# One transfer in place of four for a tile of tokens, two in place of three for a block of first weights, and the last tile stored by column halves

## The chip, the core and the metric

The kernel runs on one core of a Trainium2 chip. A core has five engines that work side by side, each from its own instruction queue in program order: TensorE (matrix products; PE and PEld in the profile), VectorE (DVE), ScalarE (ACT), GpSimd (POOL) and SyncE (SP), which here only issues transfers. Transfers between the chip's memory (DRAM) and the on-chip memory (SBUF, 128 partitions) are issued from SP's, ACT's and POOL's queues and carried out by 16 DMA engines that all queues share. Products land in PSUM, from where ScalarE and VectorE fetch them. The metric is the device time of one execution in microseconds (us), lower is better.

## What is computed

The input `x` has 2048 tokens of 576 channels. It is normalized per token, and the output is the sum of x, a state-space convolution over the tokens, and a feed-forward layer:

```python
xn = _layernorm(x, axis=-1)
return x + _A_ref(xn, A_re, A_im, B_re, B_im, C_re, C_im, log_dt, Dskip) + _B_ref(xn, w1, w2)

def _B_ref(x, w1, w2):                       # w1: 576 x 4608, w2: 4608 x 576
    h = jnp.einsum("bsd,df->bsf", x, w1)
    h = _silu(h)
    return jnp.einsum("bsf,fd->bsd", h, w2)

def _A_ref(u, A_re, ...):                    # per channel d
    K = jnp.einsum("dn,dnl,dn->dl", Cc, jnp.exp(logdA[:, :, None] * l), dB).real
    y = irfft2(rfft2(u padded) * rfft2(K padded))[..., :L]      # causal convolution of length 2048
    return y + u * Dskip
```

All of it is float32. The kernel forms float32 products from three products of rounded parts (a high half and a low half of each operand: hi x hi, hi x lo, lo x hi).

## The kernel before

**Tiles.** The 2048 tokens are 16 tiles of 128 tokens, numbered j; tile j has the tokens whose number is j modulo 16, and the token's other digits choose the partition. Two tiles (j, j + 1) make a pair, whose rows of 2 x 576 numbers are contiguous in DRAM. Tiles 0 to 7 are half 0, tiles 8 to 15 half 1; four tiles are a block b of 512 tokens.

**x.** `load_x` brings a pair in by four transfers of 32 partitions each (`quarters`), the first pair by eight, of one tile and 32 partitions each, on SP's and ACT's queues by turns. `norm` takes mean and variance on VectorE (`bn_stats`, line 188), the reciprocal root on POOL (line 193), and writes xn (line 197). `turned` and `put_xt` transpose xn on TensorE (line 122), ScalarE writes the high halves `xh` (line 123) and VectorE the low halves `xl` (line 125). xn also goes to DRAM (`dxn`, POOL, line 240), from where the convolution reads it back.

**Feed-forward.** The 4608 hidden features are chunks of 4 x 128. `load_w1` brings the 576 x 256 weights of two of them in three transfers: the rows 0 to 511 (line 257), and the last 64 rows twice, to the lower and the upper 64 partitions (lines 258 and 259). `split_w1` makes `w1h` on ScalarE (line 279) and `w1l` on VectorE (line 281); `load_w2` and `split_w2` do the same for w2 (lines 288, 297, 299). `up` forms the hidden product for one set of 128 features and one block in `ph` (lines 311 to 313), then SiLU and the two halves `gh`, `gl` (lines 319 to 321). `down` multiplies with w2 (line 341) and adds to `acc`, which holds x at first (line 346). The last blocks of half 1 are formed with fewer products (`wino_ffn`, whose weights are split at line 385).

**Convolution.** It runs as side work beside the feed-forward, a piece after each step (`weave`): normalized x is spread and transformed (`spread`, into `d1u`), the kernel K is generated from tables (`kgen`), and per frequency block both are multiplied (`spectral`) and transformed back (`conv`). In half 0 the finished tiles are stored to the output by POOL and the convolution's part is later added in DRAM by accumulating stores (`last` in `tail`). In half 1 `conv` puts its part into the same PSUM banks as `down`.

**Order.** A scheduler lays out each engine's queue from the program by its own estimate of durations, under orders that the code adds (`behind`: not ahead of a given instruction). Each queue is then served strictly in order. Buffers come from rotating pools; a transfer into a buffer waits until the buffer's last reader is done.

**The ends.** At the start, SP issues x, w1 and w2 in program order, ACT's queue carries half of the first x pair's transfers and half of the first w1 block. At the end, the pairs 8, 10 and 12 and the tiles 14 and 15 of half 1 are stored by SP and ACT, two quarters each, as their last additions finish.

Of the kernel before, what the change touches and what calls it, by code (L numbers as in the profile page):

```python
# [13 lines left out]
ALU = mybir.AluOpType  # L14
# [8 lines left out]
NJ = 16  # L23
NKT = 4
HD = D // 2
# [16 lines left out]
def kernel(  # L42
# [21 lines left out]
    nc = tc.nc  # L64
# [2 lines left out]
    WINO_C = 2  # L67


    xv = x.rearrange("b (n q2 q1 j) d -> q1 q2 n (b j) d", q2=2, q1=2, j=NJ)  # L70
    ov = out.rearrange("b (n q2 q1 j) d -> q1 q2 n (b j) d", q2=2, q1=2, j=NJ)

    def quarters(v, engines):

        for q in range(4):
            yield slice(32 * q, 32 * q + 32), v[q // 2, q % 2], engines[q % len(engines)]

    dram = ctx.enter_context(tc.tile_pool(name="dram", bufs=1, space=DRAM))
    d1u = dram.tile([32 * P, D], F32, name="d1u")
# [10 lines left out]
    s4 = None  # L90
# [19 lines left out]
    acc = {}  # L110
# [21 lines left out]
    pairs = {}  # L132
    held = []
    pins = {}
    wino = {}

    def behind(ins):
        return tc.issue_after(ins) if ins is not None else nullcontext()

    def spread(up):  # L140

        s1 = up.tile([P, 2, P], F32R, name="s1", bufs=1)
        nc.gpsimd.dma_start(s1, cs1)
        for j in range(NJ):
            src = up.tile([P, D], F32, tag="xr", name="xr")
            nc.sync.dma_start(src, dxn[:, j])
            for m in range(2):
                lo, hi = slice(64 * m, 64 * m + 64), slice(64 - 64 * m, 128 - 64 * m)
                u1 = up.tile([P, D], F32, tag="u1", name="u1")
                sp = up.tile([P, D], F32R, tag="sp", name="sp")  # L150
                nc.scalar.copy(sp[lo, :], src[lo, :])
                nc.vector.tensor_sub(sp[hi, :], src[lo, :], sp[lo, :])
                for h in range(2):
                    hs = slice(h * HD, (h + 1) * HD)
                    pu = pss.tile([P, 512], F32, tag="pss", name="pu")
                    nc.tensor.matmul(pu[:, :HD], s1[:, 0, :], sp[:, hs], start=True, stop=False)
                    nc.tensor.matmul(pu[:, :HD], s1[:, 1, :], sp[:, hs], start=False, stop=True)
                    nc.scalar.copy(u1[:, hs], pu[:, :HD])  # L158
                nc.gpsimd.dma_start(  # L159
                    d1u.rearrange("(p m j) d -> m j p d", m=2, j=NJ)[m, j], u1)  # L160
                yield j

    def load_x(j, pool, tag, engines):

        t = pool.tile([P, 2, D], F32, tag=tag, name=f"{tag}{j}")
        for i in range(j, j + 2, 1 if j == 0 else 2):
            for ps, v, eng in quarters(xv, engines):
                if j == 0:
                    eng.dma_start(t[ps, i], v[:, i])
                else:  # L170
                    eng.dma_start(t[ps], v[:, j:j + 2])
        pairs[j] = t
        return t[:, 0, :], t[:, 1, :]

    def store(t, j, engines, **more):

        for ps, v, eng in quarters(ov, engines):
            eng.dma_start(v[:, j:j + 2] if len(t.shape) > 2 else v[:, j], t[ps], **more)

    def norm(p0, js, xs):  # L180

# [60 lines left out]
    def ffn():  # L242
# [7 lines left out]
        def load_w1(half, c, t):  # L250

            f = c * FT + t
            first = half == 0 and c == 0
            r1 = (pa if first and t else w1x if t and w1x else wp).tile([P, 5, 2 * P], F32, tag="w1r", name="w1r", bufs=1)
            for eng, a, e in ((nc.scalar, 0, P), (nc.sync, P, 2 * P)) if first and t == 0 else ((nc.sync, 0, 2 * P),):
                fs = slice(f * P + a, f * P + e)
                eng.dma_start(r1[:, 0:4, a:e], w1[0:512, fs].rearrange("(k p) f -> p k f", p=P))
                eng.dma_start(r1[0:64, 4, a:e], w1[512:576, fs])
                pins["load"] = eng.dma_start(r1[64:128, 4, a:e], w1[512:576, fs]).ins
            R1[half, c, t] = r1  # L260

        def need_w1(half, c, t):
            if (half, c, t) not in R1:
                load_w1(half, c, t)

        def next_w1(half, c, t):
            new = (half, c + 1) if c + 1 < NCH else (half + 1, 0)
            if w1x and new < (1, WINO_C):
                load_w1(*new, t)
# [53 lines left out]
        def down(blk, jj, terms=None):  # L323
            half, c, b = blk
            j = 8 * half + 4 * b + jj
            js = slice(jj * P, (jj + 1) * P)
            if half == 1 and c == NCH - 1 and jj % 2 == 0:
                pools = (((ps2, "ps2"), (pss, "pss")), ((pss, "pss"),) * 2) if jj == 0 else (((ps2, "ps2"),) * 2, ((ps1, "ps1"),) * 2)
                for i in range(2):
                    begun[j + i] = [pool.tile([P, 512], F32, tag=tag, name="po") for pool, tag in pools[i]]  # L330
                conv((j, j + 1), (begun[j], begun[j + 1]))
                for i in range(2):
                    conv_load(j + i + AHEAD)
            terms = terms or [(G[blk, t], W2[half, c, t]) for t in range(FT)]
            for h in range(2):
                hs = slice(h * HD, (h + 1) * HD)
                po = begun[j][h] if j in begun else ps2.tile([P, 512], F32, tag="ps2", name="po")
                n = 0
                for gs, ws in terms:
                    for g, w in ((0, 0), (0, 1), (1, 0)):  # L340
                        pins["pe"] = nc.tensor.matmul(po[:, :HD], gs[g][:, js], ws[:, w, hs],  # L341
                                                      start=n == 0 and j not in begun, stop=n == 3 * len(terms) - 1,
                                                      skip_group_check=j in begun).ins
                        n += 1
                with tc.high_priority():
                    nc.vector.tensor_add(acc[j][:, hs], po[:, :HD], acc[j][:, hs])  # L346
            if half == 0 and c == NCH - 1:
                if j % 2:
                    store(pairs[j - 1], j - 1, (nc.gpsimd,))
                    acc[7 + j], acc[8 + j] = load_x(7 + j, accp, "acc", (nc.gpsimd,))  # L350

        def next_xt(b):
# [65 lines left out]
        for i, blk in enumerate(plain[:-1]):  # L418
            half, c, b = blk
            later = True  # L420
            new = (half, c + 1) if c + 1 < NCH else (half + 1, 0)
            more = new < (1, WINO_C)
# [559 lines left out]
    def tail():  # L982

        def last(j):
            y = yp.tile([P, 2, D], F32, tag="yt", name="yt", bufs=2)
            py = [[pool.tile([P, 512], F32, tag=tag, name="py") for pool, tag in pools]
                  for pools in (((ps2, "ps2"), (pss, "pss")), ((pss, "pss"),) * 2)]
            conv((j, j + 1), py)
            for i in range(2):
                for h in range(2):  # L990
                    nc.scalar.copy(y[:, i, h * HD:(h + 1) * HD], py[i][h][:, :HD])
                conv_load(j + i + AHEAD)
            store(y, j, (nc.gpsimd,), accum_op=ALU.add)

        steps = [(tail_at[0] + j * tail_at[1], conv_load, j) for j in range(AHEAD)]
        steps += [(tail_at[2] + j * tail_at[3], last, j) for j in range(0, 8, 2)]
        for at, f, j in sorted(steps, key=lambda v: v[0]):
            yield at
            with behind(pins["load"]):
                f(j)  # L1000
# [24 lines left out]
    def conv_load(j):  # L1025
        if j < NJ:
            yss[j] = yp.tile([P, 4, HD], F32, tag="ys", name="ys", bufs=AHEAD)
            for h in range(2):
                nc.sync.dma_start(yss[j][64 * h:64 * h + 64],
                                  d2[j * 256:(j + 1) * 256, h * HD:(h + 1) * HD].rearrange("(q r) d -> r q d", q=4))  # L1030

    def conv(js, banks):

        ys = [yss.pop(j) for j in js]
        first = pins["pe"]
        for n in range(8 * len(js)):
            i, q1, q2, h = n // 8, n // 4 % 2, n // 2 % 2, 1 - n % 2
            o = 64 * q1 + 32 * q2
            rows = slice(64 * h, 64 * h + 64)
            with tc.high_priority() if n else nullcontext(), behind(first):  # L1040
                mm = nc.tensor.matmul(banks[i][h][o:o + 32, :HD], s4[rows], ys[i][rows, 2 * q2 + q1],
                                      start=True, stop=True, tile_position=(64 * h, o), skip_group_check=True)
            if n == 0:
                first = mm.ins
# [64 lines left out]
        next(g)  # L1109
    weave(fg, 276, sd)  # L1110
    for j in range(8, 14, 2):
        store(pairs[j], j, (nc.sync, nc.scalar))
    for j in (14, 15):
        store(acc[j], j, (nc.sync, nc.scalar))


def _hi_lo(a):
# [75 lines left out]
```

## Time and profile before

| | us |
|---|---|
| median of three runs (1107.56 to 1108.49) | 1107.63 |
| the profiled execution, its own time | 1108.0 |
| its span, first to last instruction | 1106.1 |
| TensorE busy in it | 1089.5 |
| VectorE busy in it | 950.6 |
| ScalarE busy in it | 722.6 |

The profiled execution's span leaves out 1.9 us of its own time. Lines of the profile read: line of the kernel, engine, operation, tile written from tile read, shape, count, then durations. In an answer in order of time the first number is the start in us, the second the duration or the stretch of a merged group in us, and the bracket tells how long the engine had been idle before and what ended that. A q behind an engine's name (SPq, ACTq) marks the issue of a transfer; the transfer itself lands later. A row of the queues tells packets, megabytes, and the time of its packets as a share of 16 engines over the window: q1 is SP's queue, q10 ACT's, q0 POOL's.

### The profile page before, as it was taken

How to read it: one execution, taken by the hardware profiler on the slowest of the kernel's cores; microseconds unless marked ns; L12 is line 12 of the kernel's file. 1: busy time of each engine (PE TensorE's matmuls, PEld its weight loads, DVE VectorE, ACT ScalarE, POOL GpSimd, SP SyncE). 2: the span in 40 equal slices, each digit the busy share in tenths (PEclk: the TensorE clock that was granted, in tenths of full speed). 3: DMA queues.
4: the chain of work that ended last, by engine and by line, in shares of the span. 5: the costliest groups of instructions: out<-in, count | busy, mean ns of one | idle time of the engine just before them, and what ended most of it. 6: DMA issues, size and time to landing. Idle time of an engine off the chain costs nothing.

```text
span 1106.1 us, 23074 instructions
## 1 busy us (share of the span) xinstructions
PE 1089.5 (98%) x9101; PEld 986.5 (89%) x9101; DVE 950.6 (86%) x1615; ACT 722.6 (65%) x1283; POOL 141.5 (13%) x246
## 2 busy tenths in 40 slices
PE   6999999999999999999999999999999999999998
PEld 5989999898998888898999899999999998999787
DVE  6699989999999999999999997988888888886323
ACT  4475457677777676767667656877778777785320
POOL 1112100000000000000330001111111111111220
PEclk9999999999999999999999999999999999999999
DMA  8536552355263535457974246456545655554984
GB/s 261 157 123 205 168 165 94 118 149 153 84 176 108 138 125 132 154 120 254 240 196 89 84 92 193 146 167 179 158 152 176 182 173 150 177 161 109 248 216 111
DMA packets 163100, 173.67 MB, mean 157 GB/s; under 512 B 88608, under 2 KB 128816, under 8 KB 162352
## 3 DMA queue, kind: packets, MB, share of 16 engines
q1 hardware_dynamic: 137360, 105.02, 34.6%
q0 software_dynamic: 24272, 65.38, 19.4%
q10 hardware_dynamic: 1360, 1.80, 0.7%
q8 instruction: 72, 1.18, 0.5%
q14 instruction: 36, 0.29, 0.1%
HBM read 109.64 MB, written 62.60 MB: 156 GB/s over the span
## 4 chain that ended last, share of the span: by engine, by line
PE 78%; DVE 12%; ACT 3%; DMA 3%; issue 2%; SPq 0%; POOL 0%; ACTq 0%; DVEq 0%
PE po L341 34%; PE ph L311 16%; PE pb L468 6%; PE pc L468 3%; PE kp L888 2%; PE pk L1022 2%; PE pb L1022 2%; PE pu L1022 2%; PE pa L468 2%; PE ph L313 1%; PE ph L312 1%; PE z L903 1%; DMA kl<-d1k 1%; DVE acc L346 1%; DVE th L829 1%
## 5 line engine op out<-in xcount | busy, mean ns | idle before, releaser
L341 PE MATMUL po<-w,gh 128*128 128x288 f32 x2304 | 474.3, 296 | 0.7 <-DVE acc L346 0.7
L341 PEld LDWEIGHTS po<-w,gh 128*128 128x128 f32 x2304 | 375.1, 188 | 16.6 <-issue 3.3
L341 PE MATMUL po<-w,gl 128*128 128x288 f32 x1152 | 333.5, 295 | 0.0
L341 PEld LDWEIGHTS po<-w,gl 128*128 128x128 f32 x1152 | 214.9, 188 | 1.7
L346 DVE TENSOR_TENSOR acc<-po,acc 128x288 f32<-128x288 f32 x296 | 129.8, 451 | 54.5 <-PE po L341 53.2
L311 PE MATMUL ph<-xh,w1h 128*128 128x512 f32 (+1 forms) x368 | 99.7, 388 | 1.4 <-ACT gf L319 1.0
L311 PE MATMUL ph<-xl,w1h 128*128 128x512 f32 (+1 forms) x368 | 98.2, 384 | 0.0
L311 PE MATMUL ph<-xh,w1l 128*128 128x512 f32 (+1 forms) x368 | 98.0, 383 | 0.0
L319 ACT ACTIVATE gf<-ph 128x512 f32<-128x512 f32 (+1 forms) x92 | 53.0, 579 | 51.3 <-PE ph L313 31.5
L311 PEld LDWEIGHTS ph<-xl,w1h 128*128 128x128 f32 x368 | 68.0, 191 | 13.4
L311 PEld LDWEIGHTS ph<-xh,w1l 128*128 128x128 f32 x368 | 66.6, 189 | 12.0
L311 PEld LDWEIGHTS ph<-xh,w1h 128*128 128x128 f32 x368 | 65.0, 191 | 11.7 <-ACT gf L319 1.6
L845 ACT ACTIVATE c<-th,magic 128x1040 f32<-128x1040 f32 x36 | 42.0, 1168 | 40.6 <-DVE C L866 26.5
L159 POOL DMA_DIRECT2D d1u<-u x32 | 17.6, 550 | 393.9 <-ACT u L158 392.5
L847 ACT ACTIVATE c<-th 128x1040 f32<-128x1040 f32 x36 | 38.7, 1074 | 40.7 <-DVE th L846 40.6
L321 DVE TENSOR_TENSOR gl<-gf,gh 128x512 fp32r<-128x512 f32 (+1 forms) x92 | 60.3, 658 | 3.8 <-ACT gh L320 3.6
L927 POOL DMA_DIRECT2D m<-in_cm_dram x64 | 34.0, 533 | 216.0 <-PE pu L1022 135.8
L320 ACT CAST gh<-gf 128x512 fp32r<-128x512 f32 (+1 forms) x92 | 55.1, 602 | 8.7 <-PE po L341 7.7
L485 DVE TENSOR_TENSOR gl<-gf,gh 128x512 fp32r<-128x512 f32 x56 | 37.8, 688 | 23.4 <-ACT gh L484 23.0
L865 DVE TENSOR_TENSOR S<-th,C 128x1024 f32<-128x1024 f32 x36 | 43.8, 1218 | 7.4 <-ACT th L848 7.3
L846 DVE SCALAR_TENSOR_TENSOR th<-c,th 128x1040 f32<-128x1040 f32 x36 | 44.3, 1232 | 0.3 <-ACT c L845 0.3
L829 DVE TENSOR_TENSOR th<-vt,fT 128x1040 f32<-128x1040 f32 x36 | 44.3, 1233 | 0.2
(269 smaller groups left out, 2371.0 us busy)
## 6 DMA issues: line engine op xcount, KB each, us to landing
w1r<-in_B_w_dram SPq DMA_DIRECT2D x35, 512.0 KB, 3.9
dw<-w SPq DMA_DIRECT2D x28, 576.0 KB, 4.8
w<-dw POOLq DMA_DIRECT2D x28, 576.0 KB, 5.9
w2r<-in_B_w_dram SPq DMA_DIRECT2D x44, 288.0 KB, 4.8
d1u<-u POOLq DMA_DIRECT2D x32, 288.0 KB, 2.9
d1k<-stage SPq DMA_DIRECT2D x18, 512.0 KB, 6.5
ul<-d1u SPq DMA_DIRECT2D x32, 288.0 KB, 3.0
kl<-d1k SPq DMA_DIRECT2D x32, 288.0 KB, 3.6
```

The costliest lines, as they stand in the source:

```text
L311: nc.tensor.matmul(ph, w[:, kt, :], v[:, kt, a:e], start=n + kt == 0, stop=False)
L319: nc.scalar.activation(gf, ph, AF.Silu)
L320: pins["gh"] = nc.scalar.copy(gh, gf).ins
L321: pins["gl"] = nc.vector.tensor_sub(gl, gf, gh).ins
L341: pins["pe"] = nc.tensor.matmul(po[:, :HD], gs[g][:, js], ws[:, w, hs], start=n == 0 and j not in begun, stop=n == 3 * len(terms) - 1, ski ...
L346: nc.vector.tensor_add(acc[j][:, hs], po[:, :HD], acc[j][:, hs])
L468: pins["pe"] = nc.tensor.matmul(dst, a[:, kt], v[:, kt], start=start and n == 0, stop=stop and n == 5, skip_group_check=True).ins
L829: nc.vector.tensor_mul(split(th), row(vt[:, 0:65], 65), col(fT, i, 65))
L845: nc.scalar.activation(c65, th, AF.Identity, bias=magic)
L846: nc.vector.scalar_tensor_tensor(th, c65, MAGIC, th, op0=ALU.subtract, op1=ALU.subtract)
L865: nc.vector.tensor_mul(ov3, t[:, :, 0:64].rearrange("n d (x y) -> n d x y", y=32), mv3)
L1022: nc.tensor.matmul(dst, st, mv[:, hs], start=n == 0, stop=n == 3 * len(terms) - 1)
```

## The change

The token's digits are put on the partitions in another order, so that a tile or a pair is one access pattern with the four quarters q outermost, and `load_x` and `store` issue one transfer. The two copies of w1's last 64 rows become one transfer whose source repeats the rows through a leading step of 0. The convolution's scratch `d1u` and the loop of `conv` follow the new order of the quarters. The closing stores all go through ACT's queue, except that tile 15 is stored in two halves of 288 columns, by ACT and by SP.

```diff
-    xv = x.rearrange("b (n q2 q1 j) d -> q1 q2 n (b j) d", q2=2, q1=2, j=NJ)
-    ov = out.rearrange("b (n q2 q1 j) d -> q1 q2 n (b j) d", q2=2, q1=2, j=NJ)
-
-    def quarters(v, engines):
-
-        for q in range(4):
-            yield slice(32 * q, 32 * q + 32), v[q // 2, q % 2], engines[q % len(engines)]
+    xv = x.rearrange("b (n q j) d -> q n (b j) d", q=4, j=NJ)
+    ov = out.rearrange("b (n q j) d -> q n (b j) d", q=4, j=NJ)
...
                 nc.gpsimd.dma_start(
-                    d1u.rearrange("(p m j) d -> m j p d", m=2, j=NJ)[m, j], u1)
+                    d1u.rearrange("(e m q j) d -> m j e q d", m=2, q=2, j=NJ)[m, j], u1)
...
         t = pool.tile([P, 2, D], F32, tag=tag, name=f"{tag}{j}")
-        for i in range(j, j + 2, 1 if j == 0 else 2):
-            for ps, v, eng in quarters(xv, engines):
-                if j == 0:
-                    eng.dma_start(t[ps, i], v[:, i])
-                else:
-                    eng.dma_start(t[ps], v[:, j:j + 2])
+        if j == 0:
+            for i, eng in enumerate(engines):
+                eng.dma_start(t[:, i], xv[:, :, i])
+        else:
+            engines[0].dma_start(t, xv[:, :, j:j + 2])
...
-    def store(t, j, engines, **more):
-
-        for ps, v, eng in quarters(ov, engines):
-            eng.dma_start(v[:, j:j + 2] if len(t.shape) > 2 else v[:, j], t[ps], **more)
+    def store(t, j, eng, **more):
+        eng.dma_start(ov[:, :, j:j + 2] if len(t.shape) > 2 else ov[:, :, j], t, **more)
...
-                eng.dma_start(r1[0:64, 4, a:e], w1[512:576, fs])
-                pins["load"] = eng.dma_start(r1[64:128, 4, a:e], w1[512:576, fs]).ins
+                pins["load"] = eng.dma_start(r1[:, 4, a:e], w1[512:576, fs].unsqueeze(0).broadcast_to([2, 64, e - a])).ins
...
-                    store(pairs[j - 1], j - 1, (nc.gpsimd,))
+                    store(pairs[j - 1], j - 1, nc.gpsimd)
...
-            store(y, j, (nc.gpsimd,), accum_op=ALU.add)
+            store(y, j, nc.gpsimd, accum_op=ALU.add)
...
-            i, q1, q2, h = n // 8, n // 4 % 2, n // 2 % 2, 1 - n % 2
-            o = 64 * q1 + 32 * q2
+            i, q, h = n // 8, n // 2 % 4, 1 - n % 2
+            o = 32 * q
...
-                mm = nc.tensor.matmul(banks[i][h][o:o + 32, :HD], s4[rows], ys[i][rows, 2 * q2 + q1],
+                mm = nc.tensor.matmul(banks[i][h][o:o + 32, :HD], s4[rows], ys[i][rows, q],
...
     for j in range(8, 14, 2):
-        store(pairs[j], j, (nc.sync, nc.scalar))
-    for j in (14, 15):
-        store(acc[j], j, (nc.sync, nc.scalar))
+        store(pairs[j], j, nc.scalar)
+    store(acc[14], 14, nc.scalar)
+    for h, eng in enumerate((nc.scalar, nc.sync)):
+        hs = slice(h * HD, (h + 1) * HD)
+        eng.dma_start(ov[:, :, 15, hs], acc[15][:, hs])
```

Because the scheduler lays out the queues anew, three places of them are shown, before and after. Rows give the line, the operation, the tile written from what is read, and the shape of what is written; the kernel's lines are some 6 to 9 lower in the new file.

SP's queue at the start, before (w1r is the raw w1, w2r the raw w2, acc the x pairs):

```order
L169 DMA acc_104<-in_A_u_dram 32x576 x4
L257 DMA w1r<-in_B_w_dram 128x4x128
L258 DMA w1r<-in_B_w_dram 64x128
L259 DMA w1r<-in_B_w_dram 64x128
L257 DMA w1r<-in_B_w_dram 128x4x256
L258 DMA w1r<-in_B_w_dram 64x256
L259 DMA w1r<-in_B_w_dram 64x256
L171 DMA acc_171<-in_A_u_dram 32x1152 x4
L288 DMA w2r<-in_B_w_dram 128x576 x4
L171 DMA acc_252<-in_A_u_dram 32x1152 x4
L171 DMA acc_299<-in_A_u_dram 32x1152 x4
```

and with the change:

```order
L163 DMA acc_104<-in_A_u_dram 128x1x576
L249 DMA w1r<-in_B_w_dram 128x4x128
L250 DMA w1r<-in_B_w_dram 128x1x128
L249 DMA w1r<-in_B_w_dram 128x4x256
L250 DMA w1r<-in_B_w_dram 128x1x256
L165 DMA acc_162<-in_A_u_dram 128x1x1152
L279 DMA w2r<-in_B_w_dram 128x576 x4
L165 DMA acc_240<-in_A_u_dram 128x1x1152
L165 DMA acc_284<-in_A_u_dram 128x1x1152
```

The order of what is loaded is the same; each group of four is one, and each w1 block has two transfers in place of three.

VectorE's queue behind the first two tiles, before (w1l are the low halves of w1, st the statistics of the second x pair):

```order
L281 TENSOR_TENSOR w1l_185<-w1r_113,w1h_184 128x640
L281 TENSOR_TENSOR w1l_189<-w1r_113,w1h_188 128x640
L281 TENSOR_TENSOR w1l_193<-w1r_120,w1h_192 128x640
L281 TENSOR_TENSOR w1l_197<-w1r_120,w1h_196 128x640
L188 BN_STATS st_200<-acc2_171 128x6 x4
L189 BN_AGGR mv_201<-st_200 128x2 x2
```

and with the change:

```order
L272 TENSOR_TENSOR w1l_173<-w1r_107,w1h_172 128x640
L180 BN_STATS st_188<-acc2_162 128x6 x4
L272 TENSOR_TENSOR w1l_177<-w1r_107,w1h_176 128x640
L272 TENSOR_TENSOR w1l_181<-w1r_112,w1h_180 128x640
L272 TENSOR_TENSOR w1l_185<-w1r_112,w1h_184 128x640
L181 BN_AGGR mv_189<-st_188 128x2 x2
```

The statistics of the second pair now stand ahead of three of the four low halves of w1.

The end of ACT's queue, before (SP's ends in the same four rows):

```order
L484 CAST gh<-gf 128x512 x2
L178 DMA out_dram<-acc_6463 32x1152 x2
L178 DMA out_dram<-acc_6528 32x1152 x2
L178 DMA out_dram<-acc_6868 32x1152 x2
L178 DMA out_dram<-acc_7052 32x576 x4
```

and with the change, where SP's has only the second half of the last tile:

```order
L475 CAST gh<-gf 128x512 x2
L170 DMA out_dram<-acc_6412 4x32x1152
L170 DMA out_dram<-acc_6471 4x32x1152
L170 DMA out_dram<-acc_6803 4x32x1152
L170 DMA out_dram<-acc_6981 4x32x576
L1107 DMA out_dram<-acc_6981 4x32x288
```

Ten issues on each of two queues become five on ACT's and one on SP's.

## The prediction, made before the change was run

> **What bounds the kernel now.** I read the page's busy shares first, then busy time by stretches, then the order of time at both ends, then the DMA queues in short windows.
>
> ```profile
> span 1106.1 us, 23074 instructions
> PE 1089.5 (98%) x9101; PEld 986.5 (89%) x9101; DVE 950.6 (86%) x1615; ACT 722.6 (65%) x1283; POOL 141.5 (13%) x246
> ...
> core 0: us, PE busy (x) PEld busy (x) DVE busy (x) ACT busy (x) POOL busy (x), PEclk, DMA share, GB/s
> 0.00:12.00 12.00, 3.58 (x14) 2.67 (x15) 5.34 (x17) 4.50 (x9) 2.05 (x7) 1.00 0.72 204
> 12.00:30.00 18.00, 16.90 (x125) 16.22 (x125) 16.15 (x42) 9.51 (x24) 2.62 (x4) 1.00 1.01 294
> 30.00:110.00 80.00, 79.44 (x490) 71.68 (x489) 66.51 (x134) 49.07 (x75) 14.93 (x17) 1.00 0.51 161
> 110.00:510.00 400.00, 399.14 (x3998) 359.91 (x3997) 385.66 (x576) 267.70 (x404) 19.04 (x32) 1.00 0.48 141
> ...
> 1084.00:1106.10 22.10, 17.20 (x196) 14.75 (x194) 5.95 (x13) 0.00 (x0) 0.00 (x0) 0.95 0.44 109
> ```
>
> TensorE is idle 16.6 us of 1106.1: 8.4 before 12 us, 1.1 up to 30, 4.9 at the end, almost nothing between. So issue time saved on SP in the middle buys nothing: TensorE has no wait to lose there. The change can gain a few us at most, at the two ends; but whatever makes TensorE wait is added to the end in full, since it has no spare time to catch up. The loads and stores of x at the two ends are what this change rebuilds. The start, in order of time:
>
> ```profile
> 0.75 1.79 SPq L169 DMA_DIRECT2D acc<-in_A_u_dram  x4
> ...
> 4.29 0.82 DVE L188 BATCH_NORM_STATS2 st<-acc 128x6 f32<-128x288 f32 x2 [3.36 <-DMA acc<-in_A_u_dram]
> ...
> 9.59 0.72 ACT L279 CAST w1h<-w1r 128x640 fp32r<-128x640 f32 x1 [0.82 <-DMA w1r<-in_B_w_dram]
> ...
> 11.08 1.23 PE L311 MATMUL ph<-xh,w1h 128*128 128x256 f32 x4 [0.46 <-ACT xh L123]
> ...
> 15.05 1.53 DVE L188 BATCH_NORM_STATS2 st<-acc 128x6 f32<-128x288 f32 x4
> ...
> 15.54 0.64 PE L311 MATMUL ph<-xh,w1l 128*128 128x256 f32 x4
> ...
> 17.87 1.99 POOL L240 DMA_DIRECT2D dxn<-xn  x3
> ...
> 23.30 2.98 DVE L188 BATCH_NORM_STATS2 st<-acc 128x6 f32<-128x288 f32 x8
> ...
> 26.20 1.41 DVE L299 TENSOR_TENSOR w<-w2r,w 128x576 fp32r<-128x576 f32 x2
> ...
> 29.89 0.29 PE L341 MATMUL po<-w,gl 128*128 128x288 f32 x1
> ```
>
> The first statistics wait for x (3.36 us), and the first product (11.08) follows 6.8 us later. The fourth x pair is read by the statistics that end at 26.28, ahead of the low halves of w2 that TensorE needs by 29.89.
>
> **What a transfer costs.** Rows of the DMA view in the windows 0 to 0.76, 2 to 3, 44 to 54, 172 to 176.3 and 1085 to 1090 us:
>
> ```profile
> acc<-in_A_u_dram SPq DMA_DIRECT2D x1, 72.0 KB, 2.4
> ...
> q10 hardware_dynamic: 90, 0.15, 38.6%
> ...
> q1 hardware_dynamic: 1072, 2.36, 87.6%
> ...
> q1 hardware_dynamic: 688, 0.66, 49.6%
> ...
> q10 hardware_dynamic: 96, 0.30, 24.2%
> ```
>
> MB divided by (share x 16 x window) is what one busy DMA engine moves: quarters of x 24.3 GB/s, the 96-row parameter loads 16.8, w1 19.3, the closing stores 15.5. A 72 KB quarter over 16 engines (4.6 KB each) moves in 0.2 us, so 2.2 of its 2.4 us are fixed.
>
> In these rows every transfer has a DRAM pattern whose outermost count is 32, 64, 96 or 128, and the 96- and 128-row loads of 44 to 54 us keep 87.6% of all 16 engines busy, ACT's 32-row quarters alone 38.6%. The change leaves no such count: `q n (b j) d` starts with q = 4, and `unsqueeze(0).broadcast_to([2, 64, ...])` with 2. The trace shows no transfer of that kind, so I bound it from both sides: still 16 engines (nothing lost), or one share for each outermost step, 4 engines for x and the output and 2 for the last w1 rows, the same ones each time. I take the second: 32, 96 and 128 rows all divide evenly over 16 engines, as a split by outermost rows would do, and 4 steps leave such a split nothing for twelve engines.
>
> The Trainium skill's page "DMA: Bandwidth & Descriptors", section "Why a DMA increments its semaphore by 16 and not by 1", says the engine count is the largest number up to 16 that divides the outermost non-1 count of both patterns, on the lowest-numbered engines for SP and ACT. By that rule the x and output transfers run on 4 engines and the broadcast on 2, the sum below; by the rows alone 16 stays possible, 1107. No run here shows it yet.
>
> **The start.** Per engine among the narrow four at 24.3 GB/s: a 288 KB tile 3.03 us, a 576 KB pair 6.07. For w1 at 19.3: the first two half loads 0.85 (wide) + 1.70 (broadcast, two engines) each, 5.1 together; the next 1.70 + 3.39 = 5.1. Four w2 loads, wide, 3.0. SP's queue is served in order, ACT's beside it on the same engines. Landings = 0.75 + 2.2 + the sum so far: tiles 0 and 1 at 9.0 (together), w1 at 14.1 and 19.2, pair 2 at 25.3, w2 at 28.3, pair 4 at 34.4. The three stores of dxn (17.87; 1152 KB, wide) come at that point and put 3.0 more on each engine, so pair 6 lands at 43.5.
>
> First product: statistics at 9.1 for 4.29, so 15.9 for 11.08; w1's cast, ready at 14.1, is on time. Next, VectorE's new order puts pair 2's statistics ahead of the second w1 low half: 25.4 + 1.53, then 0.8 for that subtraction, so the product of 15.54 comes at 27.7, +12.2. Then the statistics of pairs 4 and 6, ahead of the w2 subtractions on the same engine: pair 6 at 43.5, half of 2.98 behind it, done at 45.1 for 26.28. **+18.8 us**, all seen by TensorE at 29.89, since it arrives there at about +12 and waits for the low parts. What comes after (parameters, xj) has its data by then: the two xj pairs and the next w1 end 17.3 us after pair 6's data, at about 60.8, while the parameters are issued at 44 + 18.8 in the new run.
>
> Saved here: two or three issues of 0.45 us on SP and ACT, 1.3 us, which lie in front of waits for data and are lost in them. The loads' fixed 2.2 us is paid once either way.
>
> **The middle.** A chunk's last w1 rows take 3.39 us on two engines in place of 0.42 on sixteen, less one issue of 0.45: they land 2.5 us later.
>
> ```profile
> L279 ACT CAST w1h<-w1r 128x640 fp32r<-128x640 f32 x44 | 30.0, 725 | 2.1 <-DMA w1r<-in_B_w_dram 2.1
> ...
> 121.86 0.60 ACT L319 ACTIVATE gf<-ph 128x512 f32<-128x512 f32 x1 [3.00 <-DVE xt L125]
> ...
> 124.40 1.36 ACT L279 CAST w1h<-w1r 128x640 fp32r<-128x640 f32 x2 [1.28 <-DMA w1r<-in_B_w_dram]
> ...
> 175.28 0.60 ACT L319 ACTIVATE gf<-ph 128x512 f32<-128x512 f32 x1 [2.50 <-PE ph L313]
> ```
>
> These 44 casts are 22 loads; where the buffer is single, about every second has its cast right behind the landing, as at 124.40. Behind a late cast on ScalarE stand the SiLU and the casts of g, which TensorE's `down` reads. But ScalarE has waits of 2.5 to 3 us of its own there, which cover most of it. Bounds for 11 loads: 0 and 27 us; I take 0.35 each, **+4**, the POOL stores and loads at the half's change and the late x pairs included. d1u's new pattern starts with 64 and costs nothing.
>
> **The end.**
>
> ```profile
> 1092.64 0.85 ACTq L178 DMA_DIRECT2D out_dram<-acc  x2
> ...
> 1084.92 17.79 SPq L178 DMA_DIRECT2D out_dram<-acc  x10
> ...
> out_dram<-acc ACTq DMA_DIRECT2D x2, 72.0 KB, 2.4
> ...
> 1101.24 0.46 DVE L346 TENSOR_TENSOR acc<-po,acc 128x288 f32<-128x288 f32 x1 [0.35 <-PE po L341]
> ```
>
> Now the last quarter is issued at 1102.4 and lands 2.4 later, 1104.8. After the change ACT's queue holds pair 10 from 1092.64: 2.2 + 6.07, pair 12 6.07, tile 14 3.03, and two halves of tile 15 at 1.52 each on the same engines (SP's half shares them): 1113.0, **+8.2**. Spread wide it would be one issue less, -0.5.
>
> **Sum.** 18.8 + 4 + 8.2 = 31.0 on the profiled execution: 1106.1 becomes 1137.1, with the 1.9 us around the span 1139.0 for its 1108.0. Against the median of the runs, 1107.63: **1138.6**. Bounds: at 16.8 GB/s per engine the start's four x terms of 6.07 and dxn's 3.0 grow by 45% (+12), and the end's 18.2 us of transfers at 15.5 GB/s by 10: 1161. Without the w1 narrowing and dxn's 3.0, the start is +9.9, the middle 0: 1126.
>
> **Rivals.** (1) Wide after all: the first tiles land at 0.75 + 2.2 + 1.5 = 4.45 for 4.17, the end gains 0.5: 1107.4, not slower. For it: one transfer's first rows are only a description, and 128 partitions stand on the other side. Decides at once: do the first statistics start before 5 us? (2) The same, and the freed queue slots also remove what TensorE idles between 12 and 110 us (1.7) and 0.7 at the end: 1105. Against it: those 1.7 us hang on ScalarE and VectorE as well. (3) Only the count of 4 is narrow, the broadcast is wide: w1 at 10.4 us of engine time, pair 6 at 37.6, start +12.9, end +8.2, middle 1: 1130. (4) Narrow and slow, 16 GB/s: 1161. (5) Wide, but VectorE's new order makes the w1 low halves wait for pair 2: with pair 2 landing at 14.45 as now, at most 3 us: 1110.
>
> The skill's same page, "Rules for kernel authors", speaks for rival 1: it advises gathering small transfers, since under 64 KB they are mostly overhead. The rows agree on the fixed part (2.2 of 2.4 us), but here it lies behind other work except at the ends; by that rule alone the time would be 1107.
>
> **Numbers.** Forecast (narrow, full engine rate) 0.53, (3) 0.12, (4) 0.15, (1) 0.12, (2) 0.05, (5) 0.03. The even split at three different counts is why narrow gets 0.8; that nothing smaller than 32 was ever tried in the trace is the 0.2. What a measurement tells from no change is about 0.2%, 2.2 us: faster 0.05, same 0.12, slower 0.83. Range 1116 to 1162: below it rivals 1, 2 and 5 (0.2), above it nearly nothing; the forecast's own range is 1126 to 1150.
>
> **What would show it.** Right: first statistics near 9 us, landings of whole x pairs of 6 us and more beyond the fixed part, TensorE idle some 19 us more before 60 us, the last store landing some 11 us after the last addition in place of 3.6. Wrong: the first statistics near 4.5 us (then the spread was wide, and the time is 1107); if they are late but the end is not, the output is spread differently; if w1 lands 4.4 us after its issue as now, the broadcast is wide.

## The result and the profile after

| | before | after |
|---|---|---|
| median of five runs, us | 1107.75 | 1191.83 (1189.41 to 1195.02) |
| span of the profiled execution, us | 1106.1 | 1191.8 |

The ratio is 1.0762, with a 95% interval from 1.0744 to 1.0779. The change costs 84 us where I had forecast 31, and the time lies above the range of 1116 to 1162. The direction and the first cause were right; one term of the sum, the middle of the kernel, was not.

The page of the changed kernel, its head:

```profile
span 1191.8 us, 22902 instructions
...
PE 1106.2 (93%) x9101; PEld 998.1 (84%) x9101; DVE 951.2 (80%) x1615; ACT 718.4 (60%) x1283; POOL 125.6 (11%) x210
```

TensorE's 9101 products are the same. Of the 85.7 us in the span, 69.0 are new idle time (1191.8 - 1106.2 = 85.6, against 16.6), and 16.7 are longer products (1106.2 against 1089.5). Where they arise is seen by counting TensorE's products in both traces and comparing the start of the same number. The two kernels do not order neighbouring products alike everywhere, so a row is good to about 1 us. The last two columns are from two experiments below: the changed kernel with x and the output in quarters again (only the broadcast is narrow), and with the broadcast undone (only x and the output are narrow).

```
product   before     after     late    only broadcast   only x/output
500         89.6     112.7    +23.1             +5.1           +16.0
1250       191.6     230.7    +39.1            +14.3           +26.8
5000       552.1     593.7    +41.6            +15.8           +26.9
6000       646.4     706.4    +60.0            +16.3           +42.9
8500      1032.9    1098.9    +66.0            +22.2           +43.1
9100      1100.9    1176.0    +75.1            +22.2           +53.7
end       1106.1    1191.8    +85.7            +21.2           +64.5
```

So the loss comes in five places: the start (23), the stage behind it (16), the change of the halves (18), the convolution's output (9) and the end (11); some 8 lie between. I had priced the start at 18.8, the end at 8.2 and everything between at 4; it measured 52.

**The transfers did become narrow.** The DMA view of the changed kernel, in the windows 33 to 36 us (a pair of x alone), 214 to 216 (a broadcast of w1's last rows alone) and 1174 to 1179 (closing stores alone). Columns: packets, MB, busy share of 16 engines.

```profile
q1 hardware_dynamic: 69, 0.31, 25.3%
...
q1 hardware_dynamic: 94, 0.10, 13.6%
...
q10 hardware_dynamic: 114, 0.51, 25.3%
```

25.3% of 16 engines is 4.0 engines, and 13.6% is 2.2, a little over the two of the pattern. MB by share gives 25.5 and 25.2 GB/s for each engine of the x and output transfers, a little more than the 24.3 I had used. The trace's packets of four bytes, counted for each queue, say the same: before, ACT's queue had 272 for 17 transfers and SP's 6064 for 379, 16 each. After, ACT's 8 transfers have 42 = 16 + 2 + 4 + 5 x 4, and SP's 310 have 4348 = 310 x 16 - 36 x 14 - 9 x 12: 36 broadcasts with 2, nine x or output transfers with 4, all others with 16. The Trainium skill, "DMA: Bandwidth & Descriptors", section "Why a DMA increments its semaphore by 16 and not by 1", says that each engine which a transfer of SP's or ACT's queue uses posts one write to the semaphore, and that the number of engines follows from the outermost counts. If the packets of four bytes are these writes, the totals of both queues (42 and 4348) agree with it.

**The start**, in order of time, answers to the rows shown of before:

```profile
2.89 5.90 SPq L249 DMA_DIRECT2D w1r<-in_B_w_dram  x1
...
11.76 0.82 DVE L180 BATCH_NORM_STATS2 st<-acc 128x6 f32<-128x288 f32 x2 [10.82 <-DMA acc<-in_A_u_dram]
...
18.54 1.23 PE L302 MATMUL ph<-xh,w1h 128*128 128x256 f32 x4 [0.46 <-ACT xh L118]
...
30.03 1.54 DVE L180 BATCH_NORM_STATS2 st<-acc 128x6 f32<-128x288 f32 x4 [9.65 <-DMA acc<-in_A_u_dram]
31.49 2.28 DVE L272 TENSOR_TENSOR w1l<-w1r,w1h 128x640 fp32r<-128x640 f32 x3
32.35 1.22 PE L302 MATMUL ph<-xh,w1l 128*128 128x256 f32 x4 [10.06 <-DVE w1l L272]
...
48.67 1.54 DVE L180 BATCH_NORM_STATS2 st<-acc 128x6 f32<-128x288 f32 x4 [4.66 <-DMA acc<-in_A_u_dram]
...
50.92 0.40 PE L332 MATMUL po<-w,gh 128*128 128x288 f32 x1 [1.85 <-DVE w L290]
...
51.15 0.36 PE L332 MATMUL po<-w,gl 128*128 128x288 f32 x1
```

Every predicted link is there: the statistics late, the low halves of w1 behind the second pair's statistics, the fourth pair last, and the product of 29.89 us at 51.15, 21.3 us late for a predicted 18.8. The sizes of the links are others than predicted. The product of 15.54 us comes at 32.35, 16.8 us late for a predicted 12.2; up to 37.58 TensorE then runs 5.2 us of products at half clock (granted clock 0.50 in that stretch), which costs an estimated half of them, 2.6; and for the low halves of w2 behind the fourth pair it waits 1.85 us (the row of 50.92), where the sum had 6.6 (18.8 - 12.2). The first row shows what I had not priced: SP's own issue of one transfer took 5.9 us, where before the first w1 transfers took 0.4 to 0.6.

**What TensorE waits for**, in the view of waits (us in total, times, longest), after, and then before:

```profile
PE po L332 <- DVE acc L337: 23.8, 10, 7.0
PE pt L117 <- DVE xn L189: 15.4, 2, 14.3
PE ph L302 <- DVE w1l L272: 10.1, 1, 10.1
PE pc L459 <- ACT w1h L376: 4.2, 1, 4.2
```

```profile
PE pt L122 <- DVE xn L197: 8.0, 2, 6.9
...
PE po L341 <- DVE acc L346: 0.7, 1, 0.7
```

The two rows on `pt` and `w1l` are the start. The largest is new: TensorE's second products wait for VectorE to add the last ones into `acc` and so to free PSUM, 23.8 us against 0.7. Two stretches of the changed kernel's order of time show why VectorE is late. The first is in the stage behind the start:

```profile
124.63 0.78 SPq L165 DMA_DIRECT2D xj<-in_A_u_dram  x1
...
136.65 0.82 DVE L180 BATCH_NORM_STATS2 st<-xj 128x6 f32<-128x288 f32 x2 [7.07 <-DMA xj<-in_A_u_dram]
137.39 0.44 DVE L337 TENSOR_TENSOR acc<-po,acc 128x288 f32<-128x288 f32 x1
...
137.88 0.85 PE L332 MATMUL po<-w,gh 128*128 128x288 f32 x2 [5.54 <-DVE acc L337]
```

A late x pair takes 12 us from its issue to its statistics (before, a quarter took 4.1 us to its landing, in the median). VectorE stands 7.07 us at its statistics, the addition waits behind them in the same queue, and TensorE waits for the addition. The second is the change of the halves:

```profile
637.50 0.67 POOL L165 DMA_DIRECT2D acc<-in_A_u_dram  x1 [12.36 <-DMA out_dram<-acc]
638.16 0.64 POOL L154 DMA_DIRECT2D d1u<-u  x1
647.78 0.70 ACT L153 COPY u<-pu 128x288 f32<-128x288 f32 x2 [13.14 <-DMA d1u<-u]
648.50 0.67 ACT L146 CAST sp<-xr 64x576 fp32r<-64x576 f32 x1
649.20 0.75 DVE L147 TENSOR_TENSOR sp<-xr,sp 64x576 fp32r<-64x576 f32 x1 [10.87 <-ACT sp L146]
649.98 0.46 DVE L337 TENSOR_TENSOR acc<-po,acc 128x288 f32<-128x288 f32 x1
650.50 0.85 PE L332 MATMUL po<-w,gh 128*128 128x288 f32 x2 [7.04 <-DVE acc L337]
```

Read upwards it is one chain over four queues: TensorE waits for an addition, which stands behind a subtraction on VectorE, which waits for a cast on ScalarE, which stands behind a copy that waits 13 us until the write of `d1u` has left its buffer, and that write stands on POOL's queue behind a narrow load, which itself waited 12.36 us for a narrow store. The write of `d1u` is wide and half the load's size; in the DMA view (window 638 to 638.5; the last number is the time to landing) it takes as long as the load in front of it:

```profile
acc<-in_A_u_dram POOLq DMA_DIRECT2D x1, 576.0 KB, 9.6
d1u<-u POOLq DMA_DIRECT2D x1, 288.0 KB, 9.5
```

The third place, the convolution's output, has such a chain on ScalarE:

```profile
1118.54 0.40 ACT L982 COPY yt<-py 128x288 f32<-128x288 f32 x1 [6.31 <-DMA out_dram<-yt]
1118.83 1.14 ACT L475 CAST gh<-gf 128x512 fp32r<-128x512 f32 x2
...
1119.87 0.62 ACT L376 CAST w1h<-w1r 128x512 fp32r<-128x512 f32 x1
...
1120.54 1.22 PE L459 MATMUL pc<-s1h,w1h 128*128 128x512 f32 x2 [4.15 <-ACT w1h L376]
```

The copy into `yt` waits 6.31 us until POOL's narrow accumulating store out of the buffer is done, a cast of w1 stands behind the copy, and TensorE waits 4.15 us for the cast: the last row of the waits above.

**The clock.** Busy time by stretches of the changed kernel (the number behind POOL is the clock granted to TensorE; before it was 1.00 from 12 to 1030 us):

```profile
30.00:50.90 20.90, 15.62 (x103) 14.74 (x103) 12.31 (x30) 7.30 (x18) 2.62 (x4) 0.82 0.46 160
50.90:58.00 7.10, 7.08 (x43) 6.91 (x43) 6.13 (x20) 3.39 (x7) 2.42 (x4) 0.76 0.25 97
...
132.00:138.00 6.00, 0.46 (x4) 0.23 (x2) 1.35 (x4) 3.23 (x4) 0.00 (x0) 0.88 0.78 282
138.00:143.00 5.00, 5.00 (x21) 5.00 (x22) 4.75 (x13) 0.00 (x0) 1.98 (x2) 0.50 0.09 38
...
650.50:656.00 5.50, 5.50 (x24) 5.39 (x24) 5.50 (x7) 4.16 (x6) 0.00 (x0) 0.56 0.22 68
```

After the wait of 5.5 us that ends at 137.88, TensorE runs 5 us at half its clock; after the 7.0 us at 650.50 likewise. That is how a wait costs more than its length. In all stretches at half clock together TensorE is busy for 28.3 us; at half speed that is an estimated 14 of the 16.7 us of longer products. The Trainium skill, "TensorE: Matmul & The Clock Gate", "Part 1: The HAM clock gate", says that an idle window of about 3.4 us halves the clock until a busy one has passed; these rows agree (0.50 and 0.56 behind waits of 5.5 and 7.0 us).

**The end**:

```profile
1160.01 0.65 ACTq L170 DMA_DIRECT2D out_dram<-acc  x1
...
1167.72 8.04 ACTq L170 DMA_DIRECT2D out_dram<-acc  x3
...
1176.32 0.46 DVE L337 TENSOR_TENSOR acc<-po,acc 128x288 f32<-128x288 f32 x1 [0.34 <-PE po L332]
1176.80 0.63 SPq L1107 DMA_DIRECT2D out_dram<-acc  x1
```

From the start of the last addition to the end of the span are 15.5 us, before 4.8 (1106.1 - 1101.24).

### The profile page after: what moved, and what is told of

It is laid out like the page before. It is cut to its first block, busy times and chain, and to the rows that moved or that the text cites. A ratio compares the mean times of both kernels' runs of the same rounds, so it can differ in the third digit from the quotient of the medians.

```text
span 1191.8 us, 22902 instructions
## 1 busy us (share of the span) xinstructions
PE 1106.2 (93%) x9101; PEld 998.1 (84%) x9101; DVE 951.2 (80%) x1615; ACT 718.4 (60%) x1283; POOL 125.6 (11%) x210
## 3 DMA queue, kind: packets, MB, share of 16 engines
q0 software_dynamic: 28304, 65.40, 17.7%
## 4 chain that ended last, share of the span: by engine, by line
PE 38%; DVE 21%; issue 18%; DMA 14%; ACT 4%; SPq 2%; POOL 1%; POOLq 0%; DVEq 0%; ACTq 0%
PE po L332 17%; PE pb L459 5%; DMA kl<-d1k 4%; PE ph L302 4%; PE pc L459 2%; DMA w2r<-in_B_w_dram 2%; DVE acc L337 2%; DMA xj<-in_A_u_dram 2%; PE pk L1013 2%; PE pu L1013 2%; DVE C L845 2%; DVE gl L312 2%; DVE th L820 1%; DMA w<-dw 1%; DMA d1u<-u 1%
## 5 line engine op out<-in xcount | busy, mean ns | idle before, releaser
L332 PE MATMUL po<-w,gh 128*128 128x288 f32 x2304 | 483.7, 300 | 29.4 <-DVE acc L337 23.8
L332 PEld LDWEIGHTS po<-w,gh 128*128 128x128 f32 x2304 | 381.9, 191 | 48.0 <-DVE acc L337 26.4
L332 PE MATMUL po<-w,gl 128*128 128x288 f32 x1152 | 337.3, 298 | 0.0
L332 PEld LDWEIGHTS po<-w,gl 128*128 128x128 f32 x1152 | 218.1, 191 | 1.8
L836 ACT ACTIVATE c<-th,magic 128x1040 f32<-128x1040 f32 x36 | 42.0, 1166 | 40.9 <-DVE C L857 24.3
L998 DVE TENSOR_TENSOR kl<-kl,kh 128x576 fp32r<-128x576 f32 x32 | 24.2, 757 | 26.4 <-ACT kh L997 24.0
```

The source lines that it names most:

```text
L836: nc.scalar.activation(c65, th, AF.Identity, bias=magic)
```

## The experiments

Each kernel is the changed one with the edit shown, unless it says otherwise. The edits are shortened to the lines that matter. Theory A is the narrow transfers; the ratios are to the kernel before in the same session, with their 95% intervals.

**x and the output in quarters again (e1), and the broadcast alone undone (e2).**

```diff
+        for q in range(4):      # e1: load_x, store and the closing stores; first pair on SP and ACT by turns
+            eng.dma_start(t[32 * q:32 * q + 32], xv[q][:, j:j + 2])
```
```diff
+                eng.dma_start(r1[0:64, 4, a:e], w1[512:576, fs])      # e2
+                pins["load"] = eng.dma_start(r1[64:128, 4, a:e], w1[512:576, fs]).ins
```

> All loads of x and all stores of the output go back to four transfers of 32 partitions, on the queues of the kernel before; the broadcast of the last w1 rows stays. Theory A (a transfer is spread over as many engines as its outermost DRAM count allows: 4 for x and the output, 2 for the broadcast; nearly all of the +84 us is the 4): about 1118 us (1110 to 1128), x quarters land within 3 to 6 us again, some 13 to 16 packets at once. Rival B (the broadcast on two engines holds up everything behind it on SP's queue): above 1150. Rival C (the width of the transfers doesn't matter, VectorE's and the convolution's new order does): about 1190, as changed.

> Only the broadcast is undone: the last 64 rows of w1 are loaded by two transfers again; x and the output stay at one transfer. Theory A: 1170 to 1187, since the x transfers on four engines remain. Rival B: below 1140. Rival C: about 1190.

Measured: 1129.9 us (ratio 1.0199, 1.0184 to 1.0214) and 1172.65 (1.0575, 1.0549 to 1.0601). Each part alone is slower than before, by 21.9 and 64.6 us against the 1108.05 of the same session; together 86, about the 84 of the whole. Theory A holds for x, B and C fall; but the broadcast costs twice the 10 that A gave it (1118), just outside A's range.

**Late pairs by two transfers (e3), and by four (e4).**

```diff
-            engines[0].dma_start(t, xv[:, :, j:j + 2])
+                for q in range(2):      # e3, for the late pairs alone
+                    engines[0].dma_start(t[64 * q:64 * q + 64], xv[2 * q:2 * q + 2][:, :, j:j + 2])
+                for q in range(4):      # e4, the same place
+                    engines[0].dma_start(t[32 * q:32 * q + 32], xv[q][:, j:j + 2])
```

> The four late x pairs (xj) alone are loaded by two transfers of 64 partitions, whose outermost DRAM count is 2, in place of one with the count 4. Theory A: each runs on two engines, about 2 packets at once in place of 4, a pair needs 12 us of transfer in place of 6, VectorE's statistics of xj wait longer, and the time rises by 6 to 25 us, to 1198 to 1217. A spread by bytes or by partitions, or a fixed four engines for each transfer: the same 4 packets at once or more, and 1180 to 1193.

> The four late x pairs (xj) alone are loaded by four transfers of 32 partitions. Theory A with the loss placed by stages (+16 us between 112 and 190 us, where VectorE waits 7 us for xj and the addition that frees TensorE's PSUM stands behind): 1176 (1170 to 1182), and the 5.5 us wait of TensorE at 138 us is gone. If the late w1 blocks cause that stage's loss: 1185 to 1192.

Measured: 1220.35 and 1187.52 us. In the first, a stretch with a late pair alone (the DMA view, 66 to 70 us):

```profile
q1 hardware_dynamic: 46, 0.20, 12.3%
```

That is 2.0 engines of 16: the same bytes in two transfers in place of one run on half the engines, and the kernel loses 28.5 us more, 3 beyond my upper figure. It is the sharpest test of the rule: smaller transfers, and more of them, but half the engines. The time of e4 lies where I had put it if late w1 blocks made that stage's loss (1185 to 1192), not at A's 1176. Its quarters remove TensorE's 5.5 us wait at 138 us and bring 6.4 us up to product 1250 (+32.7 in place of +39.1), but only 4.3 at the end; I had expected 16. The rest of that stage's loss is there with the broadcast alone (+9.2 between products 500 and 1250).

**Quarters in one place each**: the half's change (e5), the convolution's output (e6), the closing stores (e7), and the start (e10).

```diff
+        if eng is nc.gpsimd and not more:      # e5: four transfers; load_x likewise for j >= 8; e6: if more
-        store(pairs[j], j, nc.scalar)          # e7: quarters on SP and ACT by turns
+            if tag == "acc" and j < 8:         # e10: four transfers; the first pair by eight
```

> Only the four stores of finished pairs and the four loads of the second half's x at the half's change (GpSimd's queue, 570 to 650 us) go back to four transfers of 32 partitions. Theory A with the loss placed by stages (+18.5 us there, the d1u writes of the u stage stand behind the narrow transfers on GpSimd's queue, ScalarE's next u copy waits up to 13 us for one, VectorE and TensorE behind it): 1174 (1169 to 1180), and TensorE's waits of 4.9 and 7.0 us at 611 and 650 us are gone. If that stage's loss comes from the late w1 or from the changed order: 1186 or more.

> Only the four accumulating stores of yt (GpSimd's queue, 1050 to 1160 us) go back to four transfers of 32 partitions. Theory A: the loss of 9 us between 1100 and 1140 us goes, 1183 (1179 to 1187), and TensorE's waits of 4.2 us at 1120 and 2.3 us at 1131 are gone. If the loads of ys or w1 make those waits: 1189 to 1195.

> Only the closing stores (pairs 8, 10, 12, tiles 14 and 15) go back to four transfers of 32 partitions on SP's and ScalarE's queues. Theory A: the time from the last addition to the end falls from 14.9 us to about 4.4: 1181 (1178 to 1184). If HBM or the order of the queues sets the end: above 1187.

> Only the loads of the first eight x tiles (before 30 us) go back to transfers of 32 partitions; late x pairs, output and broadcast stay as changed. Theory A: TensorE is 5 to 8 us behind the kernel before at 90 us in place of 23, since only the broadcast is narrow there, and the time is 1176 (1171 to 1180). If the broadcast sets the start: 1186 or more.

Measured: 1174.14, 1183.15, 1184.12 (four runs from 1176.66 to 1186.52) and 1178.12 us. The first, second and fourth are as expected, and each removes the waits of its own place. In the third the end behind the last addition falls from 15.5 to 4.1 us (1174.9 - 1170.74) in its profiled run, which is the fastest of the four; the median lies just above the range of 1178 to 1184. The undone places give 13.7 (start), 4.3 (late pairs), 17.7 (half), 8.7 (output) and 7.7 us (end), in sum 52; undoing all at once gives 62. The start is worth 18.9 us at product 500 (+4.2 in place of +23.1, somewhat better than the 5 to 8 expected) and 15.6 in the span at the end: some of what arrives earlier meets later narrow transfers.

**d1u on another queue (e8).**

```diff
-                nc.gpsimd.dma_start(
+                nc.scalar.dma_start(
                     d1u.rearrange("(e m q j) d -> m j e q d", m=2, q=2, j=NJ)[m, j], u1)
```

> All x and output transfers stay narrow as changed; the 32 d1u writes are issued on ScalarE's queue in place of GpSimd's. If the half's stage loses its time because d1u stands behind narrow transfers in GpSimd's queue: the waits of TensorE at 611 and 650 us shrink by more than half and the time is 1178 (1172 to 1185), some of it given back by 32 issues of about 0.6 us on ScalarE. If d1u is late because it shares the DMA engines with them, or the narrow transfers themselves are what TensorE waits for: 1190 or more.

Measured: 1188.8 us, outside both expectations. Between the products 5000 and 6000 the loss is 9.3 us in place of 18.4, and the wait at 650 us is gone, so half of that stage was the place of `d1u` on POOL's queue. What is left of it is a new wait of TensorE, of 7.6 us at 623 us, for w2. Of this kernel, in order of time, and then the same cast of the changed kernel:

```profile
587.91 14.92 SPq L862 DMA_DIRECT2D d1k<-stage  x1
...
602.92 9.96 SPq L249 DMA_DIRECT2D w1r<-in_B_w_dram  x1
...
621.69 0.67 ACT L288 CAST w<-w2r 128x576 fp32r<-128x576 f32 x1 [9.29 <-DMA w2r<-in_B_w_dram]
```

```profile
621.16 0.67 ACT L288 CAST w<-w2r 128x576 fp32r<-128x576 f32 x1 [3.56 <-DMA w2r<-in_B_w_dram]
```

SP's queue holds the loads of w1 and w2 back in both kernels (11.5 us for the w1 issue of the changed one, at 597.05), and this w2 arrives within 0.6 us of the same time in both. TensorE, no longer held by `d1u`, comes earlier and waits for it longer. Moving one victim to another queue uncovers the next one while the narrow transfers stay.

**Everything in quarters, the rest of the change kept** (e9: the two edits of e1 and e2 together; the last tile by halves, each in quarters).

> Every x load and output store in quarters of 32 partitions and the last w1 rows by two transfers, while the rest of the change stays: the new order of the quarters, the new pattern of the d1u writes, the convolution's new order, and the last tile stored by halves (each half in four quarters). Theory A: nothing but the transfers' outermost counts costs time, 1107.5 (1105.5 to 1110), so that the 84 us are the counts of 4 and 2 alone. If the new order or the pattern costs or gains something: below 1105 or above 1112.

Measured: 1107.47 us (eleven runs) against 1108.42 us, ratio 0.9993 (0.9984 to 1.0002). The new order of quarters, the convolution's order, the pattern of `d1u` and the halves cost nothing that can be told, and gain nothing.

**Why the broadcast costs 22 us.** On top of e9, a transfer that nobody reads is added behind each w1 load, narrow (e11) or wide (e12), and again with its place held (e13, e14).

```diff
+                nc.sync.dma_start(spare, w1[512:576, fs].unsqueeze(0).broadcast_to([2, 64, e - a]))    # e11, e13
+                nc.sync.dma_start(spare, w1[512:576, fs].unsqueeze(1).broadcast_to([64, 2, e - a]))    # e12, e14
```

> As with everything in quarters (1107.5), so that w1 itself arrives by wide transfers, plus one additional transfer right behind each w1 load that nobody reads: the same 64 rows of w1 as a broadcast with the outermost count 2, into a spare piece of DRAM. It asks where the 22 us of the broadcast alone came from, of which I had priced 9. If from what stands behind the broadcast on SP's queue and on its two DMA engines (w2, the other loads): 1118 or more. If from w1's own late landing: 1107 to 1111.

> The same spare transfer with the two outer loops of its pattern exchanged, so that its outermost count is 64: the same bytes and rows, on 16 engines. Both explanations: 1107 to 1111 (one more issue of 0.45 us on SP, 0.4 us of the engines). More than that would mean that the additional transfer as such costs, not its width.

Measured: 1228.06 and 1134.03 us, both far off. The trace shows a fault of the experiment: since nobody waits for the spare transfers, the scheduler put all 37 into the first 230 us (136 in the wide case), each waiting at the head of SP's queue for the one before (in the narrow case they stand some 5.5 us apart), as they shared one target. It says nothing on the question. The next pair holds each in its place (`with behind(pins["load"])`) and gives it a target of its own.

> The run of the spare broadcast again, with each spare transfer held to its place right behind its w1 load in SP's queue and with a piece of DRAM of its own, so that none waits for another. w1 itself arrives wide. If the broadcast's cost comes from what stands behind it on SP's queue and on its two DMA engines (the next w1 load, w2, xj, kl): 1116 to 1130, near the 1129.9 of the broadcast alone. If it comes from the late landing of w1 itself: within 4 us of the run with the wide spare.

> The same with the loops exchanged, outermost count 64, 16 engines: 1107 to 1111. More would be the price of an additional transfer as such, to be taken off the narrow one's.

Measured: 1132.95 (1126.55 to 1134.54) and 1112.77 us (1112.14 to 1113.38). The first is 3 above the range that I had given to what stands behind the broadcast, and far outside the 4 us of the other explanation. The added transfer as such costs about 5, 2 more than I allowed; its narrowness costs 20 more, although nobody waits for its data. ScalarE's waits for w1 are 3.4 us in e13, against 13.6 in e1. So nearly all of the 22 us can come about without w1's own transfer being narrow, by what stands behind the broadcast on SP's queue and on its two engines; how the two causes share the 22 in e1 itself, where w1 is late too and the broadcast goes to SBUF and not to DRAM as the spare one does, these runs do not tell.

## Why the prediction was right or wrong

**The mechanism was right.** One transfer is spread by the outermost count of its pattern: 4, 2, and in e3 2 again, each seen as a share of the 16 engines, with x and the output at 25 GB/s for each. Rivals (1), (2) and (5) fall with the first statistics at 11.76 us; (4) falls because the engines ran at their full rate; (3) falls because the broadcast alone costs 22.

**The start** was right in the order of its links. That its sum is only 2.5 us short (21.3 for 18.8) is partly luck: the first links were 4.6 us too small (16.8 for 12.2) and the clock's 2.6 were left out, while the last wait was 4.8 too large (1.85 for 6.6). The sum let tiles 0 and 1 land at 9.0 us; their statistics start at 11.76. By the trace's packets w1's rows of 512 bytes move from 3.7 us on and the last row of the two tiles at 10.6, by turns and not one after the other. The second pair's statistics are at 30.03 for a predicted 25.4, behind SP's slow issues.

**The end** was right in kind and mis-sized: 10.7 for 8.2. ACT's queue in the DMA view of the changed kernel, from 1161.3 to 1182 us and from there to 1190.4:

```profile
q10 hardware_dynamic: 370, 1.67, 24.2%
...
q10 hardware_dynamic: 290, 0.54, 17.2%
q1 hardware_dynamic: 123, 0.14, 4.5%
```

Four engines nearly all the time at first (3.9 of 16); then 2.8 for ACT's queue and 0.7 for SP's half of tile 15, 3.5 together. By the packets of four bytes the last transfer of ACT's queue is through on two engines at 1187.7 us and on the other two at 1190.3, so the four do not end together as the sum had it. From the end of pair 8, at 1169.8, to 1190.3 the transfers took 20.5 us, where the sum had 18.2.

**The middle is the step that failed**: "Bounds for 11 loads: 0 and 27 us; I take 0.35 each, **+4**, the POOL stores and loads at the half's change and the late x pairs included." It measured 52. Four things were wrong in it.
- The bounds were made from w1's loads alone, and the rest "included" without a row. The half's change (18 us), the convolution's output (9) and the late x pairs each had a queue behind them that I did not look at: `d1u` behind POOL's stores, the additions that free PSUM behind the statistics on VectorE. The cover that I named was ScalarE's own waits; but the waits reached TensorE over VectorE's additions, and at the output over a cast on ScalarE itself that stands behind a copy.
- The bounds count 22 blocks of w1, those cast at line 279. The 14 blocks cast at line 385 were left out; in the column of the broadcast alone 5.9 us arise behind product 6000.
- For w1 I priced the lateness of its own rows. That was right in size (from the first issue of a block to its last packet, in the median of 35 blocks, 6.9 us in e1 and 4.8 before: 2.1 for a predicted 2.5), but e13 against e14 shows 20 us with w1 itself on 16 engines. What stands behind a narrow transfer pays, and I had priced none of it.
- Each long wait was counted once. With the clock it counts for more: products are longer by 16.7 us over the whole, an estimated 14 of them at half clock.

**The range** failed with it: its upper end varied the engines' rate at both ends and left the middle at 4. A range that took 27 for w1 in place of 4, and 6 us for the narrow store and 6 for the narrow load of each of the four pairs at the half (48), would have reached 1210 and held the result; that is hindsight.

**What stays open**: how the 8 us between the places, and the 5 of the added wide transfer, come about in detail; and whether one transfer of 128 partitions with a wide pattern would gain anything. With q as the slow digit of the partition, the pattern as it is written here starts with 4; another order or another layout of the tokens, which would need another convolution, was not tried. No version here beats the kernel before.

## What to carry to other kernels

Before merging transfers, write down the outermost count of both patterns: four transfers whose pattern starts with 32 run on 16 engines, one whose pattern starts with 4 runs on 4, however many partitions it fills. Price a slow transfer not by its own readers but by each queue in which something stands behind it or behind whoever waits for it, and follow that chain until it reaches the engine that bounds the kernel. On a TensorE that is 98% busy, saved issues have little to win (it was idle for 16.6 of 1106.1 us here), and a wait of 5 to 7 us costs its length and then about 5 us at half clock.

## What the hardware showed that I had not expected

- Beside narrow transfers the issuer is held up: SP needed 5.9, 8.4 and 11.5 us for single issues (at 2.89, 18.30 and 597.05 us) where 0.3 to 0.6 is usual and the longest was 4.6 before and 4.5 with everything in quarters (e9). Each delayed every later transfer in its queue, wide ones too. What holds the issue is not shown.
- The narrow transfers of POOL's queue made it carry more packets with 36 fewer transfers: 28304 against 24272, all of the increase packets of 4 and 8 bytes.
- Half clock after waits of 5.5 and 7.0 us, for about 5 us each, on a core that keeps its full clock from 12 to 1030 us in the kernel before.
